# Forgetting attention and a tanh-shrink layer: q and k loaded six tokens to a partition, one DMA per tensor, and turned from there in 96x128 blocks

## The chip, the core and the metric

The kernel runs on one core of a Trainium2 chip. A core has five engines, each with an instruction queue of its own that is worked off in order: TensorE (PE in the profile; its weight loads are shown apart as PEld), VectorE (DVE), ScalarE (ACT), GpSimd (POOL) and SyncE (SP), which here only issues DMA transfers. Engines wait for one another by semaphores. Sixteen DMA engines move the data between HBM, the large memory, and SBUF, the on-chip memory of 128 partitions. TensorE writes its results into PSUM, a small memory in banks, from which VectorE and ScalarE read them.

The metric is the device time of one execution in microseconds (us). Lower is better.

## The reference

There are two parts. The first is causal attention for 8 batches of 8 heads, with 576 tokens of 64 numbers in each head; every token has a forget value f, whose logarithms are summed along the tokens and enter the scores:

```python
scores = scale * np.matmul(q, k.transpose(0, 1, 3, 2))
log_f = np.log(np.clip(f, 0.0001, 1.0))
cum = np.cumsum(log_f, axis=-1)
decay = cum[:, :, :, None] - cum[:, :, None, :]
scores = np.where(causal, -1000000000.0, scores + decay)
scores = scores - np.max(scores, axis=-1, keepdims=True)
attn = np.exp(scores)
attn = attn / (np.sum(attn, axis=-1, keepdims=True) + 1e-09)
return np.matmul(attn, v).astype(np.float32)
```

The second takes the eight heads of a token as one row of 512 numbers, 4608 tokens in all:

```python
h = x @ w_in             # 512 x 2048
g = h - np.tanh(h)
return g @ w_out         # 2048 x 512
```

All inputs and the output are float32.

## The kernel before, in words

**Attention.** The heads are worked two at a time: pair c of batch b holds heads 2c and 2c+1, and there are 32 pairs. For each pair there are seven score tiles (`scores`, matmul at L352), kept transposed: the keys stand on the partitions and the queries along the row. A score matmul multiplies a 128-column piece of `KT` (the weights) with columns of `QT`. Both tiles have 67 rows: 64 for the head's numbers and three that carry the forget sums, so that the decay comes out of the same matmul. `QT` is [67, head, 576 tokens], `KT` the same with padding to 640. There are two of each, one for even batches and one for odd. A score tile goes to one of two PSUM banks, ScalarE turns it into exponentials `e` (L361), and GpSimd zeroes what lies above the diagonal (L371). A matmul with the values (`values`, L389) gives both the sums and the weighted values, and VectorE divides them (L398 to L400) into `xn`. SP turns `xn` by DMA transposes (L423, L425) into `XR`, where the rows of x stand with the 512 numbers on the partitions.

**The layer.** Tiles of 512 tokens, u = 0 to 8. `mlp1` is 16 steps for each tile: four matmuls of `win` with `XR` (L451) into a bank `hps`, on ScalarE the tanh of -h into one of two buffers `th` (L456), and on VectorE the sum of both, `gq` (L462). `mlp2` multiplies g with w_out. From tile 1 on this is done by seven products of quarters in place of eight; their operands are sums of quarters of g, made by VectorE (`sums`, L484), and of w_out (`weights`, L278, once). The products are matmuls at L517.

**The order.** All five queues are written out by hand, in the order in which the program issues. For pair p the function `att_items` makes a list of items: the seven score tiles with what belongs between them, and at each place (p, item) the entries that a table `LOADS` has there. Steps of the layer, seven or eight a pair, are dealt out evenly between these items. So the place in `LOADS` sets where a load, a transpose or a copy stands in its engine's queue.

**How q and k come in.** They lie in HBM as [batch, head, token, 64] in float32, and are needed with the 64 numbers on the partitions, in 16 bits. Batches 0 to 2 go another way than the others: `load_qk` (L102) puts six tokens one behind the other on each of 96 partitions, TensorE turns them into PSUM (L298), and copies place them from there (L309 on ScalarE, L311 on VectorE). These copies handle even and odd tokens apart, and write every second column.

From batch 3 on (`FAR = 3`), these are the steps, for each of q and k:

- `load_block` (L108), five times: GpSimd issues a DMA that puts 128 tokens (at last 64) on the partitions, one token of all eight heads to a partition, and turns float32 into 16 bits on the way. Each of its pieces is one token of one head, 64 numbers or 256 bytes in HBM.
- `turn_block` (L113), five times: SP issues a DMA transpose of such a block. In the result, `TQ` or `TK` ([128, 4, 576]), the two heads of a pair stand on partitions 0 to 63 and 64 to 127, and the tokens along the row in their order. There are two tiles `TQ`, and one `TK`.
- `place`: copies of 64 partitions into `QT` and `KT`. For K they are four copies on VectorE (L120) of two heads each: heads 0 and 2, then 1 and 3, then 4 and 6, then 5 and 7. For Q, ScalarE copies heads 0 to 3 one at a time (L118), and VectorE heads 4 and 6, then 5 and 7 (L120). A copy reads and writes 576 tokens in a row.

The places of the copies are these lines, where b is the batch that the copies are for, p0 is the first pair of the batch ahead of it, and p0 + 4 the first pair of batch b:

```python
on_k = (p0 + 3, 0), (p0 + 3, 2), (p0 + 4, 1), (p0 + 4, 4)
if b == FAR:
    on_k = (p0 + 3, 2), (p0 + 3, 4), (p0 + 4, 0), (p0 + 4, 4)
```

For batches 4 to 7 the first two K copies thus stand at items 0 and 2 of the pair ahead of the batch, for batch 3 at items 2 and 4. The Q copies of ScalarE stand at items 3 to 6 of the first pair of the batch before (for batch 3: 1 to 4 of the pair just ahead), and those of VectorE one pair later at items 1 and 3.

Of the kernel before, what the change touches and what calls it, by code (L numbers as in the profile page):

```python
# [17 lines left out]
FAR = 3  # L18
# [3 lines left out]
def kernel(  # L22
# [10 lines left out]
    nc = tc.nc  # L33
    P = 128

    B, H, S, D = q.shape
    NH = B * H
    DM, DFF = moe_w_in.shape
# [3 lines left out]
    NJ = 5  # L42
    NT6 = 6
# [32 lines left out]
    def keep():  # L76
        while M_AT[0] % 3 in KEPT:
            M_AT[0] += 1
        KEPT.append(M_AT[0] % 3)
# [11 lines left out]
    qraw = [qkp.tile([P, H * S * D // (S // NT6)], FP16, tag=f"qn{i}", name=f"qn{i}") for i in range(2)]  # L91
    kraw = [qkp.tile([P, H * S * D // (S // NT6)], FP16, tag=f"kn{i}", name=f"kn{i}") for i in range(2)]
    qn, kn = ([t[0:S // NT6, :].rearrange("p (h n d) -> p h n d", h=H, n=NT6) for t in raw] for raw in (qraw, kraw))
    qb, kb = ([t[:, 0:NJ * DM].rearrange("p (n e) -> p n e", n=NJ) for t in raw] for raw in (qraw, kraw))
    vn = [qkp.tile([P, NJ, H, VW], FP16, tag=f"vn{i}", name=f"vn{i}") for i in range(2)]
    QT = [qkp.tile([D + 3, H, S], FP16, tag=f"QT{i}", name=f"QT{i}") for i in range(2)]
    KT = [qkp.tile([D + 3, H, PITCH], FP16, tag=f"KT{i}", name=f"KT{i}") for i in range(2)]
    TQ = [qkp.tile([P, NPAIR, S], FP16, tag=f"TQ{i}", name=f"TQ{i}") for i in range(2)]
    TK = qkp.tile([P, NPAIR, S], FP16, tag="TK", name="TK")
# [3 lines left out]
            out=dst[b % 2][:, h0:h1, :, :].rearrange("p h n d -> p h (n d)"),  # L103
            in_=src[b, h0:h1, :, :].rearrange("h (p n) d -> p h (n d)", n=NT6))

    def load_block(dst, src, b, n):
        pn = min(P, S - n * P)
        nc.gpsimd.dma_start(out=dst[b % 2][0:pn, n, :].rearrange("p (h d) -> p h d", h=H),  # L108
                            in_=src[b, :, n * P:n * P + pn, :].rearrange("h p d -> p h d"))

    def turn_block(dst, src, b, n):
        pn = min(P, S - n * P)
        nc.sync.dma_start_transpose(out=dst[:, :, n * P:n * P + pn], in_=src[b % 2][0:pn, n, :])  # L113

    def place(dst, src, b, a, c, n, eng):
        to, of = dst[b % 2][0:D, 2 * c + a:2 * c + a + 2 * n - 1:2, 0:S], src[a * D:(a + 1) * D, c:c + n, :]
        if eng == "A":
            nc.scalar.activation(out=to, in_=of, func=AF.Copy)  # L118
        else:
            (nc.gpsimd if eng == "P" else nc.vector).tensor_copy(out=to, in_=of)  # L120

    def load_v_rest(b):
        nc.gpsimd.dma_start(out=vn[b % 2][0:S % P, NJ - 1, :, 0:D],
# [115 lines left out]
    def add(where, fn, *args):  # L239
        LOADS.setdefault(where, []).append(lambda: fn(*args))  # L240

    for b in range(2, B):
        p0 = (b - 1) * NPAIR
        at_q = [(p0 - 2, n + 2) for n in range(NJ)]
        at_k = [(p0, n) for n in range(NJ)]
        at_v = [(p0 + (1 if b >= FAR else 2), n) for n in range(NJ)]
        to_q, to_k = (p0 - 1, 1), (p0 + 1, 4)
        on_q = p0
        on_k = (p0 + 3, 0), (p0 + 3, 2), (p0 + 4, 1), (p0 + 4, 4)
        if b == FAR:  # L250
            at_q = [(p0 - 1, n + 1) for n in range(NJ)]
            to_q, on_q = (p0, 4), p0 + 3
            on_k = (p0 + 3, 2), (p0 + 3, 4), (p0 + 4, 0), (p0 + 4, 4)
        add((p0, 0), load_aug, b)
        for n in range(NJ):
            if n < NJ - 1:
                add(at_v[n], load_v_block, b, n, 0, H)
            else:
                add(at_v[n], load_v_rest, b)
            if b < FAR:  # L260
                continue
            add(at_q[n], load_block, qb, q, b, n)
            add(at_k[n], load_block, kb, k, b, n)
            add(to_q, turn_block, TQ[b % 2], qb, b, n)
            add(to_k, turn_block, TK, kb, b, n)
        if b < FAR:
            add((p0, 2), load_qk, qn, q, b, 0, H)
            add((p0, 5), load_qk, kn, k, b, 0, H)
            continue
        for n, (c, a) in enumerate(((0, 0), (0, 1), (2, 0), (2, 1))):  # L270
            add(on_k[n], place, KT, TK, b, a, c, 2, "V")
            add((on_q, (1 if b == FAR else 3) + n), place, QT, TQ[b % 2], b, a, c // 2, 1, "A")
            if c:
                add((on_q + 1, 1 + 2 * a), place, QT, TQ[b % 2], b, a, c, 2, "V")

    def weights(o, x, y, n):
        ks = slice(n * NK // 2, (n + 1) * NK // 2)
# [160 lines left out]
    def widen(n):  # L438
        turn_of[:] = [n, 0]
# [218 lines left out]
    for p in range(len(pairs) + 1):  # L658
        b, c = divmod(p, NPAIR)
        items = att_items(p)  # L660
        take = TAKE[p] if p < len(TAKE) else 8 - (p - len(TAKE)) % 2
        if p == 2 * NPAIR - 1:
            keep()
        if p == 2 * NPAIR + 1:
            KEPT.clear()
            widen(1)
        mine = mlp[at:at + take]
        at += take
        first = 15 if p == NPAIR else 0
        if p == len(pairs):  # L670
            for fn, *args in mine[0:2]:
                fn(*args)
            mine = mine[2:]
        given, n = 0, 0
        whole = sum(counts for _, counts in items)
        for emit, counts in items:
            emit()
            n += counts
            while n > first and given < len(mine) and given * (whole - first) < (n - first) * len(mine):
                fn, *args = mine[given]  # L680
                fn(*args)
                given += 1
    widen(2)
    for fn, *args in mlp[at:]:
        fn(*args)
# [28 lines left out]
```

## Time and profile before

| | |
|---|---|
| median of 3 runs | 338.77 us (338.75 to 339.58) |
| span of the profiled execution | 337.1 us |
| busy: TensorE | 330.0 us (98%) |
| busy: VectorE | 260.8 us (77%) |
| busy: ScalarE | 233.2 us (69%) |
| busy: GpSimd | 163.2 us (48%) |
| DMA queue of GpSimd's transfers | 94528 packets, 18.37 MB, 75.5% of the 16 engines' span |
| DMA queue of SP's transfers | 52892 packets, 19.89 MB, 32.4% |
| granted TensorE clock | 9 tenths or more in each of 40 slices |

The busy share is the time in which an engine works at something, as a part of the span. The rest is waiting. In a row of a timeline the columns are the start (us from the span's start), the length, the engine, the line and operation, the tile written and the tiles read, and how many instructions the row joins; in brackets stands how long the engine had been idle just before, and what released it. A row of groups has the line, the engine, the operation with its shapes (partitions x elements) and its count, then the busy time and the mean in ns of one, then the idle time just ahead of such instructions and what ended most of it. In a row of the chain of waits the first two numbers are start and length.

### The profile page before, as it was taken

The page shows a single profiled execution, that of the slowest core. Times are in us where ns is not written, and L with a number is a line of the kernel's source. Part 1 is how long each engine was busy: PE and PEld are TensorE (multiplying, and loading weights), DVE is VectorE, ACT ScalarE, POOL GpSimd, SP SyncE. Part 2 cuts the span into 40 slices and gives each one's busy share as a digit, 9 for nine tenths or more (in the row PEclk, how much of TensorE's full clock was granted, in tenths as well). Part 3 has the DMA queues.
Part 4 walks back from the last instruction along what each step waited for, and adds up shares of the span by engine and source line. Part 5 has one row for each costly group of instructions (what it writes and reads, how often), then busy time and mean ns, then how long its engine had stood idle before and what let it go on. Part 6 is the DMA issues. An engine that isn't in the chain of part 4 may idle for free.

```text
span 337.1 us, 8726 instructions
## 1 busy us (share of the span) xinstructions
PE 330.0 (98%) x3313; PEld 235.6 (70%) x3313; DVE 260.8 (77%) x509; ACT 233.2 (69%) x438; POOL 163.2 (48%) x321
## 2 busy tenths in 40 slices
PE   8899999999999999999999999999999999999996
PEld 8775558875687558845888888656865686486485
DVE  7998986659887886778867896788668866966865
ACT  6997777978977886788677867787558733632630
POOL 8977467775667564767377637722322210000000
PEclk9999999999999999999999999999999999999999
DMA  9999999999979997999899999990130022002003
GB/s 113 143 203 202 186 198 165 184 159 172 142 87 190 136 134 72 164 152 139 94 122 187 118 112 117 163 132 18 51 113 2 19 65 97 2 31 95 0 12 116
DMA packets 147468, 38.82 MB, mean 115 GB/s; under 512 B 128181, under 2 KB 146335, under 8 KB 147426
## 3 DMA queue, kind: packets, MB, share of 16 engines
q0 software_dynamic: 94528, 18.37, 75.5%
q1 hardware_dynamic: 52892, 19.89, 32.4%
q8 instruction: 26, 0.43, 0.6%
q14 instruction: 16, 0.13, 0.2%
q10 hardware_dynamic: 6, 0.01, 0.0%
HBM read 36.85 MB, written 9.44 MB: 137 GB/s over the span
## 4 chain that ended last, share of the span: by engine, by line
PE 90%; DVE 7%; ACT 2%; issue 1%; ACTq 0%
PE hps L451 36%; PE ops L517 29%; PE ps L352 11%; PE av L389 8%; PE ops L492 4%; DVE KT L311 2%; DVE QT L311 1%; PE t L298 1%; ACT e L361 1%; DVE xn L400 1%; DVE gq L462 0%; DVE TQ L187 0%; ACT th L456 0%; PE x L417 0%; DVE clo L190 0%
## 5 line engine op out<-in xcount | busy, mean ns | idle before, releaser
L451 PE MATMUL hps<-XR,win 128*128 128x512 f16 (+1 forms) x640 | 140.7, 357 | 0.3 <-DVE gq L462 0.3
L456 ACT ACTIVATE th<-hps 128x512 f32<-128x512 f32 x144 | 86.6, 602 | 55.5 <-PE hps L451 53.5
L361 ACT ACTIVATE e<-ps 128x512 f16<-128x512 f32 x192 | 110.2, 597 | 8.9 <-PE ps L352 7.4
L462 DVE TENSOR_TENSOR gq<-hps,th 128x512 f16<-128x512 f32 x144 | 98.0, 687 | 23.6 <-ACT th L456 22.0
L371 POOL TENSOR_SCALAR_AFFINE_SELECT e<-e 128x128 f16<-128x128 f16 x168 | 60.7, 364 | 71.5 <-ACT e L361 68.7
L451 PEld LDWEIGHTS <-win 128*128 128x128 f16 x640 | 57.7, 97 | 49.0 <-issue 1.1
L352 PE MATMUL ps<-QT,KT 67*128 67x64 f16 (+4 forms) x384 | 76.5, 276 | 2.0 <-DVE KT L311 1.4
L517 PEld LDWEIGHTS <-gq 128*128 128x128 f16 x640 | 60.3, 97 | 11.1
L517 PE MATMUL ops<-wout,gq 128*128 128x256 f16 x512 | 63.2, 272 | 0.0
L352 PEld LDWEIGHTS <-KT 67*128 67x128 f16 x384 | 36.4, 98 | 23.4 <-DVE KT L311 2.0
L389 PEld LDWEIGHTS <-e 128*128 128x128 f16 x896 | 32.3, 97 | 3.6
L389 PE MATMUL av<-vn,e 128*128 128x65 f16 x896 | 33.6, 193 | 0.0
L517 PE MATMUL ops<-W,sq 128*128 128x256 f16 x256 | 31.2, 272 | 0.0
L131 POOL DMA_DIRECT2D vn<-in_v_dram x32 | 28.0, 877 | 6.5 <-DMA win<-in_moe_w_in_dram 2.9
L400 DVE TENSOR_TENSOR xn<-av,rs 128x640 f16<-128x640 f32 x32 | 26.4, 825 | 1.3 <-DVE rs L399 0.2
L517 PEld LDWEIGHTS <-sq 128*128 128x128 f16 x256 | 24.1, 97 | 3.4
L108 POOL DMA_DIRECT2D kn<-in_k_dram x25 | 21.2, 848 | 2.1 <-issue 1.8
L108 POOL DMA_DIRECT2D qn<-in_q_dram x25 | 21.2, 848 | 1.8 <-issue 1.4
L371 POOL TENSOR_SCALAR_AFFINE_SELECT el<-el 128x128 f16<-128x128 f16 x28 | 9.3, 333 | 26.1 <-ACT el L361 25.8
L398 DVE TENSOR_SCALAR rs<-av 128x10 f32<-128x10 f32 x32 | 5.2, 163 | 18.2 <-PE av L389 17.0
L532 ACT ACTIVATE m<-ops 128x512 f32<-128x512 f32 x16 | 9.5, 596 | 10.9 <-PE ops L517 10.9
L484 DVE TENSOR_TENSOR gq<-gq 128x512 f16<-128x512 f16 x32 | 17.1, 533 | 0.0
(83 smaller groups left out, 311.8 us busy)
## 6 DMA issues: line engine op xcount, KB each, us to landing
out_dram<-ost SPq DMA_DIRECT2D x34, 256.0 KB
vn<-in_v_dram POOLq DMA_DIRECT2D x24, 128.0 KB, 6.2
qn<-in_q_dram POOLq DMA_DIRECT2D x20, 128.0 KB, 5.0
kn<-in_k_dram POOLq DMA_DIRECT2D x20, 128.0 KB, 5.6
win<-in_moe_w_in_dram POOLq DMA_DIRECT2D x2, 1024.0 KB, 11.8
wout<-in_moe_w_out_dram POOLq DMA_DIRECT2D x2, 1024.0 KB, 15.6
XR<-xn SPq DMA_TRANSPOSE x56
qn<-in_q_dram POOLq DMA_DIRECT2D x6, 144.0 KB, 4.6
```

What stands on the lines that cost most here:

```text
L108: nc.gpsimd.dma_start(out=dst[b % 2][0:pn, n, :].rearrange("p (h d) -> p h d", h=H), in_=src[b, :, n * P:n * P + pn, :].rearrange("h p d - ...
L131: nc.gpsimd.dma_start(out=vn[b % 2][:, n, h0:h1, 0:D], in_=v[b, h0:h1, n * P:(n + 1) * P, :].rearrange("h p d -> p h d"))
L352: nc.tensor.matmul(out=ps[:, col:col + n], lhsT=kt[0:rows, h, j * P:(j + 1) * P], rhs=qt[0:rows, h, i0:i0 + n], start=True, stop=cut == 0)
L361: nc.scalar.activation(out=e[:, lo:hi], in_=ps[:, lo:hi], func=AF.Exp, bias=-SHIFT, scale=qscale)
L371: nc.gpsimd.affine_select(out=view, in_=view, compare_op=ALU.is_ge, fill=0.0, base=0, pattern=pat, channel_multiplier=-1)
L389: nc.tensor.matmul(out=av[:, a, ib, :], lhsT=E.pop((b, c, a, j, ib)), rhs=vn[b % 2][:, j, 2 * c + a, 0:D + 1], start=(j == 0), stop=(j == ib))
L400: nc.vector.tensor_tensor(out=xn.rearrange("p i (a d) -> p a i d", a=2), in0=av[:, :, :, 0:D], in1=rs.to_broadcast([P, 2, NJ, D]), op=ALU. ...
L451: nc.tensor.matmul(out=hps[:, o:o + n], lhsT=win[:, ci, ft * P:(ft + 1) * P], rhs=XR[:, ci, t:t + n], start=(ci == 0), stop=(ci == NCH - 1))
L456: nc.scalar.activation(out=th, in_=hps, func=AF.Tanh, scale=-1.0)
L462: nc.vector.tensor_tensor(out=GQ[(u, i)][:, half, kt, :], in0=hps, in1=th, op=ALU.add)
L484: nc.vector.tensor_tensor(out=LHS[name](u, i)[:, ks], in0=LHS[x](u, i)[:, ks], in1=LHS[y](u, i)[:, ks], op=op)
L517: nc.tensor.matmul(out=ps[:, m, :], lhsT=LHS[lhs](u, kt // 4)[:, kt % 4, m * P:(m + 1) * P], rhs=rhs[:, kt, :], start=(fresh and (apart or ...
```

## The change

For batches 3 to 7, q and k are now loaded as in batch 2: `load_qk` for all eight heads, one DMA for each tensor. Each of its pieces is six tokens of one head, 1536 bytes in HBM, and it ends on 96 partitions of a raw tile, with (head, token of six, number) along the row.

`turn_raw` (L109 of the new kernel) then issues two DMA transposes for each tensor, one for heads 0 to 3 and one for heads 4 to 7. Each turns twelve blocks of 96 partitions by 128 columns. A block holds two neighbouring tokens (64 numbers each) of one head, so in `TQ` and `TK` the even tokens now stand on partitions 0 to 63 and the odd ones on 64 to 127, and the row of a head is three stretches of 96 (one for each of the three pairs of tokens among the six).

`place` takes one parity e of the tokens, of as many heads as it is told. For each stretch element it reads one of each of the three stretches, 96 elements apart, and writes them to every second column of `QT` or `KT`. The count of copies and of elements in each is as before, with other shares: K's four copies on VectorE (L118) are now the even tokens of heads 0 to 3, the odd tokens of heads 0 to 3, then the same of heads 4 to 7. ScalarE's four Q copies (L116) are even and odd of heads 0 and 1, then of heads 2 and 3; VectorE's two are even and odd of heads 4 to 7. The places of the copies in `LOADS` are the same as before. The loads have one place where they had five.

```diff
-    def load_block(dst, src, b, n):
-        pn = min(P, S - n * P)
-        nc.gpsimd.dma_start(out=dst[b % 2][0:pn, n, :].rearrange("p (h d) -> p h d", h=H),
-                            in_=src[b, :, n * P:n * P + pn, :].rearrange("h p d -> p h d"))
-
-    def turn_block(dst, src, b, n):
-        pn = min(P, S - n * P)
-        nc.sync.dma_start_transpose(out=dst[:, :, n * P:n * P + pn], in_=src[b % 2][0:pn, n, :])
-
-    def place(dst, src, b, a, c, n, eng):
-        to, of = dst[b % 2][0:D, 2 * c + a:2 * c + a + 2 * n - 1:2, 0:S], src[a * D:(a + 1) * D, c:c + n, :]
+    def blocks(t):
+        return t.rearrange("p c (g r) -> p (c g) r", r=S // NT6)
+
+    def turn_raw(dst, src, b, h0, h1):
+        nc.sync.dma_start_transpose(out=blocks(dst)[:, 3 * h0:3 * h1, :],
+                                    in_=src[b % 2][0:S // NT6, h0 * NT6 * D:h1 * NT6 * D])
+
+    def place(dst, src, b, h0, h1, e, eng):
+        to = dst[b % 2][0:D, h0:h1, e:S:2].rearrange("d h (r g) -> d h r g", g=NT6 // 2)
+        of = blocks(src)[e * D:(e + 1) * D, 3 * h0:3 * h1, :].rearrange("d (h g) r -> d h r g", g=NT6 // 2)
...
-        at_q = [(p0 - 2, n + 2) for n in range(NJ)]
-        at_k = [(p0, n) for n in range(NJ)]
...
-            at_q = [(p0 - 1, n + 1) for n in range(NJ)]
...
+        at_q, at_k, to_q, to_k = (p0 - 2, 2), (p0, 1), (p0 - 1, 1), (p0 + 1, 4)
...
+            at_q, at_k, to_q, to_k = (p0 - 1, 2), (p0, 1), (p0, 4), (p0 + 1, 4)
...
-        for n, (c, a) in enumerate(((0, 0), (0, 1), (2, 0), (2, 1))):
-            add(on_k[n], place, KT, TK, b, a, c, 2, "V")
-            add((on_q, (1 if b == FAR else 3) + n), place, QT, TQ[b % 2], b, a, c // 2, 1, "A")
-            if c:
-                add((on_q + 1, 1 + 2 * a), place, QT, TQ[b % 2], b, a, c, 2, "V")
+        add(at_q, load_qk, qn, q, b, 0, H)
+        add(at_k, load_qk, kn, k, b, 0, H)
+        for n in range(2):
+            add(to_q, turn_raw, TQ[b % 2], qraw, b, 4 * n, 4 * n + 4)
+            add(to_k, turn_raw, TK, kraw, b, 4 * n, 4 * n + 4)
+        for n in range(4):
+            m, e = divmod(n, 2)
+            add(on_k[n], place, KT, TK, b, 4 * m, 4 * m + 4, e, "V")
+            add((on_q, (1 if b == FAR else 3) + n), place, QT, TQ[b % 2], b, 2 * m, 2 * m + 2, e, "A")
+            if m:
+                add((on_q + 1, 1 + 2 * e), place, QT, TQ[b % 2], b, 4, H, e, "V")
```

In the fences below each row is one instruction, or as many as its count says: the line, the operation, the tile written and those read, and the shape; a number behind a tile's name tells apart tiles that share a name. The orders of TensorE and ScalarE are the same in both kernels, but for the line numbers and the shapes of ScalarE's copies.

VectorE around the first scores of batch 3, before. `KT_106` is the K tile of odd batches, the rows from `rs` to `xn` are the division of the pair before, and `sq` are sums of quarters of g:

```order
L120 COPY KT_106<-TK 64x2x576
L398 TENSOR_SCALAR rs<-av 128x10
L399 RECIPROCAL rs<-rs 128x10
L400 TENSOR_TENSOR xn<-av,rs 128x2x5x64
L484 TENSOR_TENSOR sq<-gq 128x512 x4
L484 TENSOR_TENSOR sq<-sq,gq 128x512
L120 COPY KT_106<-TK 64x2x576
```

and after:

```order
L118 COPY KT_106<-TK 64x4x288
L395 TENSOR_SCALAR rs<-av 128x10
L396 RECIPROCAL rs<-rs 128x10
L397 TENSOR_TENSOR xn<-av,rs 128x2x5x64
L481 TENSOR_TENSOR sq<-gq 128x512 x4
L481 TENSOR_TENSOR sq<-sq,gq 128x512
L118 COPY KT_106<-TK 64x4x288
```

The order is the same. What a copy holds has changed: two whole heads before, one parity of four heads after.

GpSimd around the load of q for a batch, before. `qn_97` is the raw tile of q for even batches, and the rows at L371 zero what lies above the diagonal in the exponentials:

```order
L108 DMA qn_97<-in_q_dram 128x8x64
L371 AFFINE_SELECT el_137<-el_137 128x128
L108 DMA qn_97<-in_q_dram 128x8x64
L371 AFFINE_SELECT e<-e 128x128
L108 DMA qn_97<-in_q_dram 128x8x64
L371 AFFINE_SELECT e<-e 128x128
L108 DMA qn_97<-in_q_dram 128x8x64
L371 AFFINE_SELECT e<-e 128x2x128
L108 DMA qn_97<-in_q_dram 64x8x64
```

and after, from the same place:

```order
L101 DMA qn_97<-in_q_dram 96x8x384
L368 AFFINE_SELECT el_137<-el_137 128x128
L368 AFFINE_SELECT e<-e 128x128 x2
L368 AFFINE_SELECT e<-e 128x2x128
L368 AFFINE_SELECT e<-e 128x128 x2
```

The whole load now stands where the first of its five parts stood, and the other four places are empty.

SP around the transposes of q for an odd batch (`TQ_108`), with those of `XR` ahead of and behind them, before:

```order
L425 DMA_TRANSPOSE XR<-xn 128x64
L113 DMA_TRANSPOSE TQ_108<-qn_98 128x4x128 x4
L113 DMA_TRANSPOSE TQ_108<-qn_98 128x4x64
L423 DMA_TRANSPOSE XR<-xn 128x4x128
L425 DMA_TRANSPOSE XR<-xn 128x64
```

and after:

```order
L422 DMA_TRANSPOSE XR<-xn 128x64
L109 DMA_TRANSPOSE TQ_108<-qn_98 128x12x96 x2
L420 DMA_TRANSPOSE XR<-xn 128x4x128
L422 DMA_TRANSPOSE XR<-xn 128x64
```

Two transposes stand where five stood. Each of them waits for the one load.

More of the change, by code (lines that the diff above doesn't have):

```diff
@@ L93 @@
     qn, kn = ([t[0:S // NT6, :].rearrange("p (h n d) -> p h n d", h=H, n=NT6) for t in raw] for raw in (qraw, kraw))
-    qb, kb = ([t[:, 0:NJ * DM].rearrange("p (n e) -> p n e", n=NJ) for t in raw] for raw in (qraw, kraw))
     vn = [qkp.tile([P, NJ, H, VW], FP16, tag=f"vn{i}", name=f"vn{i}") for i in range(2)]
@@ L119, in place @@
         else:
-            (nc.gpsimd if eng == "P" else nc.vector).tensor_copy(out=to, in_=of)
+            nc.vector.tensor_copy(out=to, in_=of)
     def load_v_rest(b):
@@ L243 @@
         p0 = (b - 1) * NPAIR
-        at_q = [(p0 - 2, n + 2) for n in range(NJ)]
-        at_k = [(p0, n) for n in range(NJ)]
[L246 to L250, printed above, removed]
-            at_q = [(p0 - 1, n + 1) for n in range(NJ)]
-            to_q, on_q = (p0, 4), p0 + 3
-            on_k = (p0 + 3, 2), (p0 + 3, 4), (p0 + 4, 0), (p0 + 4, 4)
+        late_b = b >= FAR
+        at_v = [(p0 + (1 if late_b else 2), n) for n in range(NJ)]
         add((p0, 0), load_aug, b)
@@ L259 @@
                 add(at_v[n], load_v_rest, b)
[L260 to L266, printed above, removed]
+        if not late_b:
             add((p0, 2), load_qk, qn, q, b, 0, H)
@@ L269 @@
             continue
-        for n, (c, a) in enumerate(((0, 0), (0, 1), (2, 0), (2, 1))):
-            add(on_k[n], place, KT, TK, b, a, c, 2, "V")
-            add((on_q, (1 if b == FAR else 3) + n), place, QT, TQ[b % 2], b, a, c // 2, 1, "A")
-            if c:
-                add((on_q + 1, 1 + 2 * a), place, QT, TQ[b % 2], b, a, c, 2, "V")
+        at_q, at_k, to_q, to_k = (p0 - 2, 2), (p0, 1), (p0 - 1, 1), (p0 + 1, 4)
+        on_q = p0
+        on_k = (p0 + 3, 0), (p0 + 3, 2), (p0 + 4, 1), (p0 + 4, 4)
+        if b == FAR:
+            at_q, at_k, to_q, to_k = (p0 - 1, 2), (p0, 1), (p0, 4), (p0 + 1, 4)
+            on_q = p0 + 3
+            on_k = (p0 + 3, 2), (p0 + 3, 4), (p0 + 4, 0), (p0 + 4, 4)
+        add(at_q, load_qk, qn, q, b, 0, H)
[9 more added lines that the diff above has]
+                add((on_q + 1, 1 + 2 * e), place, QT, TQ[b % 2], b, 4, H, e, "V")
     def weights(o, x, y, n):
@@ L682 @@
                 given += 1
+        assert given == len(mine)
     widen(2)
```

## The prediction

> **What bounds the kernel now.** I read the page's busy shares first, then the chain that ended last, then the windows of one batch, and then the timelines at the places where the edited copies stand.
>
> ```profile
> PE 330.0 (98%) x3313; PEld 235.6 (70%) x3313; DVE 260.8 (77%) x509; ACT 233.2 (69%) x438; POOL 163.2 (48%) x321
> 108.79 1.73 PE hps L451 x8
> 281.69 13.81 PE hps L451 x64
> 130.90:166.30 35.40, 35.40 (x347) 24.25 (x346) 27.29 (x56) 26.52 (x53) 22.36 (x43) 1.00 1.45 133
> 166.30:201.80 35.50, 35.50 (x411) 30.47 (x409) 27.28 (x56) 26.52 (x53) 22.32 (x43) 1.00 1.47 131
> ```
>
> The first row is the page's, the next two are pieces of the chain, the last two are windows of one batch each (length, then the busy time of PE, PEld, DVE, ACT and POOL, the granted clock, the DMA engines' share in them, GB/s). TensorE is busy in all of both batches, at clock 1.00, and not only nominally: eight 512-column matmuls in the middle of attention take 1.73 us (216 ns each), and 64 of them at the end, with no attention beside them, 13.81 us (216 ns each). TensorE is at its pace; nothing that the change lightens (loads, GpSimd's issues) stands in front of it. So I look for what could make TensorE wait. VectorE is idle for 8.1 us of a batch and ScalarE for 8.9 us, and both stand in TensorE's loops.
>
> **The change part by part.** Loads: 50 issues (25 a tensor) on GpSimd become 10, and the transposes on SP fall from 50 to 20. Both engines get time back, which is worth nothing where TensorE doesn't wait for them. What the change adds is in the placing copies, as many as before (30 on VectorE, 20 on ScalarE) with the same number of elements, but now reading steps of 96 elements and writing every second element.
>
> ```profile
> L120 DVE COPY KT<-TK 64x1152 f16<-64x1152 f16 x20 | 9.4, 470 | 0.3
> L311 DVE COPY QT<-t 64x576 f16<-64x576 f16 x18 | 14.4, 800 | 2.2 <-PE t L298 2.1
> L311 DVE COPY KT<-t 64x288 f16<-64x288 f16 x4 | 1.9, 477 | 0.1
> L419 DVE COPY XR<-x 128x576 f16<-128x576 f16 x2 | 0.9, 456 | 0.6 <-PE x L417 0.5
> L118 ACT ACTIVATE QT<-TQ 64x576 f16<-64x576 f16 x20 | 13.7, 683 | 0.5
> L309 ACT ACTIVATE QT<-t 64x576 f16<-64x576 f16 x4 | 3.3, 817 | 0.1
> L421 ACT ACTIVATE XR<-x 128x576 f16<-128x576 f16 x2 | 1.3, 654 | 0.0
> ```
>
> These are groups by line and shape (busy, mean ns). No row shows the new form, from SBUF with both steps; L311 and L309 have the same steps, from PSUM.
>
> *VectorE's copy.* L311 gives (800 - 477) / 288 = 1.12 ns an element and 154 ns fixed. At that pace 1152 elements take 1.44 us, the upper end. The old copy's 0.47 us, where steps cost nothing, is the lower end. It moves 1152 / (470 - 154) = 3.6 elements in a ns, four times L311's pace. [...] I take the middle of 0.80 and 1.44, 1.12 us, since L311 is the nearest in form and L120 in place: 0.67 us more than the 0.44 to 0.46 us that a single copy takes in the timelines below.
>
> [...]
>
> *ScalarE's copy.* Steps cost 817 - 654 = 163 ns for 576 elements out of PSUM (L309 against L421). I add that to L118's 0.68: 0.85 us. The lower end is 0.68; the upper is VectorE's ratio for the same two tiles, 800 / 456 = 1.75, hence 1.20 us. I take 0.85, the row of the same engine and shape.
>
> Term 1, **the first scores of batch 3**. Before, one copy placed all tokens of heads 0 and 2, and the next all of heads 1 and 3. Now one places the even tokens of heads 0 to 3 and the next the odd tokens, so head 0 needs both. VectorE's timeline, and TensorE's row with that score (the last of the x3):
>
> ```profile
> 91.22 0.69 DVE L462 TENSOR_TENSOR gq<-hps,th 128x512 f16<-128x512 f32 x1 [0.73 <-ACT th L456]
> 91.83 0.44 DVE L120 COPY KT<-TK 64x1152 f16<-64x1152 f16 x1
> 92.20 0.15 DVE L398 TENSOR_SCALAR rs<-av 128x10 f32<-128x10 f32 x1
> ...
> 93.38 1.51 DVE L484 TENSOR_TENSOR sq<-gq 128x512 f16<-128x512 f16 x4
> 94.81 0.41 DVE L484 TENSOR_TENSOR sq<-sq,gq 128x512 f16<-128x512 f16 x1
> 95.24 0.46 DVE L120 COPY KT<-TK 64x1152 f16<-64x1152 f16 x1
> 94.68 0.71 PE L352 MATMUL ps<-QT,KT 67*128 67x320 f16 x3
> ```
>
> The score starts at 94.68 + 0.71 - 0.38 = 95.01, before the second copy even begins. With the first copy 0.67 longer, the gq ahead of it up to 0.16 later (it waits for ScalarE, which has a stepped copy ahead), and nothing idle in between, the second begins at 96.07, ends at 97.19, and the score follows perhaps 0.1 later (the weight load and the hop): a wait of 2.3 us. With unchanged copies it is 95.70 + 0.1 - 95.01 = 0.8; with 0.80 us copies 1.6; with 1.44 us copies 2.9. TensorE's queue is in order, so all behind it waits too, and no later idle time can give it back. In batches 4 to 7 the table of places has both copies of the first heads two items earlier. VectorE's second one and TensorE's row with the first score of batch 5:
>
> ```profile
> 161.33 0.46 DVE L120 COPY KT<-TK 64x1152 f16<-64x1152 f16 x1
> 165.52 0.60 PE L352 MATMUL ps<-QT,KT 67*128 67x320 f16 x3
> ```
>
> [...]
>
> Term 2, **ScalarE between the scores of a batch's first pair** (batches 4 to 7, once each). Four Q copies stand there between the exponentials:
>
> ```profile
> 136.01 0.68 ACT L118 ACTIVATE QT<-TQ 64x576 f16<-64x576 f16 x1
> 136.86 0.60 ACT L361 ACTIVATE e<-ps 128x512 f16<-128x512 f32 x1 [0.17 <-PE ps L352]
> 137.48 0.68 ACT L118 ACTIVATE QT<-TQ 64x576 f16<-64x576 f16 x1
> 138.07 0.57 ACT L361 ACTIVATE e<-ps 128x512 f16<-128x512 f32 x1
> 138.67 0.68 ACT L118 ACTIVATE QT<-TQ 64x576 f16<-64x576 f16 x1
> 139.26 0.57 ACT L361 ACTIVATE e<-ps 128x512 f16<-128x512 f32 x1
> 139.86 0.68 ACT L118 ACTIVATE QT<-TQ 64x576 f16<-64x576 f16 x1
> 140.45 1.70 ACT L361 ACTIVATE e<-ps 128x512 f16<-128x512 f32 x3
> 139.89 0.38 PE L352 MATMUL ps<-QT,KT 67*128 67x448 f16 x2
> 141.07 0.38 PE L352 MATMUL ps<-QT,KT 67*128 67x320 f16 x2
> ```
>
> Score tiles have two banks, so each score waits for the exponential two before it. The exponential of 139.26 ends at 139.83 and the score starts at 139.89; the first of 140.45 ends near 141.02 (0.57 us as its neighbours) and the score starts at 141.07. TensorE is already on ScalarE's heels there. The copy at 136.01 has 0.17 us of idle time behind it and swallows its 0.16; the other three arrive in full: 4 batches x 3 x 0.163 = 2.0 us. Ends: 0, and 4 x 3 x 0.51 = 6.1 us. Batch 3's Q copies fall in front of term 1's wait and are covered by it.
>
> Term 3, **Q copies between the sums of g**:
>
> ```profile
> 146.41 0.46 DVE L120 COPY QT<-TQ 64x1152 f16<-64x1152 f16 x1
> 146.90 1.43 DVE L462 TENSOR_TENSOR gq<-hps,th 128x512 f16<-128x512 f32 x2
> 148.09 0.60 ACT L456 ACTIVATE th<-hps 128x512 f32<-128x512 f32 x1
> ```
>
> The th at 148.09 takes the buffer that the first of these gq reads (two buffers). That gq ends near 147.59; 0.67 later is 148.26, so ScalarE starts up to 0.2 late and hands it to the next score. Four batches give 0.7 us. The other VectorE copies have the 8.1 us of idle time a batch against 6 x 0.67 = 4.0 us, and I cost them at nothing; were they 1.35 us longer each, that cover would be gone. Ends: 0, and 2 us with 1.44 us copies.
>
> The DMA side I cost at nothing. The first block of q that now becomes the whole load was issued at 117.14 for a copy that stands at 136.01:
>
> ```profile
> 117.14 0.89 POOL L108 DMA_DIRECT2D qn<-in_q_dram  x1 [0.41 <-issue]
> qn<-in_q_dram POOLq DMA_DIRECT2D x1, 576.0 KB, 14.6
> qn<-in_q_dram POOLq DMA_DIRECT2D x6, 144.0 KB, 4.6
> ```
>
> A quarter of such a load lands in 4.6 us. The one of 14.6 us was issued right behind a megabyte of weights, which isn't there later. Somewhere from 6 to 9 us is my estimate between these rows, so SP waits a few us at each Q transpose; behind it in its queue stand XR's transposes, issued a pair later.
>
> Sum: 2.3 + 2.0 + 0.7 = 5.0 us. The profiled span of 337.1 becomes 342.1. The median of the runs shown is 338.77, 1.67 us above the span, and becomes 343.8 us, 1.5% slower. I count 0.3% (1.0 us) as what a measurement of this kernel can tell from no change.
>
> **The rivals.**
> A: ScalarE pays 1.75 as VectorE does out of PSUM, copies near 1.20 us. Term 2 is 6.1, term 1 some 0.3 larger: 338.8 + 9.4 = 348.2. For it, the ratio of L311 to L419; against it, L309 itself at 817.
> [...]
> B: steps are free, copies stay at 0.46 and 0.68. Then only 0.8 us of term 1 is left: 339.6, no change that can be told. It decides as long as all copies together add under 0.2 us to terms 1 to 3. For it, the old copies are in SBUF; against it, every stepped row is slower than its plain neighbour.
> [...]
> D: the load lands as late as 14.6 us. 117.14 + 14.6 and a transpose of 2 to 6 us passes 136.01 by up to 2 us, in four batches: about 352. Against it, the weights ahead of that row.
> E: fewer DMAs free something that TensorE waits for. TensorE has no gap to give from 100 us on; at most 1 us, 338.
>
> **How the numbers follow.** The forecast with its own range of 341.5 to 346 (0.80 to 1.44 us copies) has 0.53; A 0.21, B 0.09, C 0.08, D 0.04, E 0.02, something unnamed and slower 0.03. The predicted time is the forecast's 343.8. The range goes from 340.3 (1.6 us: term 1 with 0.80 us copies and ScalarE's free) to 349.8 (A with 1.44 us copies gives 2.9 + 6.1 + 2.0 = 11.0): it leaves out B, C, D and E, and takes most of A. Faster 0.02 (E), same 0.09 (B), slower 0.89.
>
> **What would show it.** In the profile after: VectorE's placing copies at 0.8 to 1.4 us and ScalarE's near 0.85; one wait of TensorE for VectorE's KT copy near 95 us, 1.6 to 2.9 long, and none like it in later batches; L352's waits for L361 grown by half a us at the first pair of batches 4 to 7; GpSimd's busy time some 35 us less, with no use. The prediction is wrong if the copies stay under 0.5 us, if ScalarE's pass 1 us, if TensorE waits for XR or a transpose, or if the wait at 95 us is missing.

## The result, and the profile after

The changed kernel takes 342.06 us (median, 342.02 to 343.02), against 338.77 before: 1.0101 times as long, with an interval of 1.0085 to 1.0117. The profiled execution has a span of 340.3 us, 3.2 more than before.

First the page of the kernel after: TensorE's busy time, GpSimd's, the score matmuls (the last entry is the idle time ahead of them and what ended most of it), the placing copies, and from the groups by shape VectorE's copies of Q.

```profile
PE 332.0 (98%) x3313; PEld 236.8 (70%) x3313; DVE 269.7 (79%) x509; ACT 235.8 (69%) x438; POOL 133.5 (39%) x281
q0 software_dynamic: 55488, 18.36, 52.7%
L349 PE MATMUL ps<-QT,KT 67*128 67x64 f16 (+4 forms) x384 | 76.6, 276 | 3.0 <-DVE KT L118 1.5
L116 ACT ACTIVATE QT<-TQ 64x576 f16<-64x576 f16 x20 | 17.1, 853 | 0.5
L118 DVE COPY KT<-TK 64x1152 f16<-64x1152 f16 x20 | 16.8, 842 | 0.3
L118 DVE COPY QT<-TQ 64x1152 f16<-64x1152 f16 x10 | 8.3, 830 | 0.2
```

GpSimd has 30 us less to do (35 were forecast), and its DMA queue takes 52.7% of the engines' span where it took 75.5%. Nobody was waiting for either. The copies have grown from 0.47 to 0.84 us on VectorE and from 0.68 to 0.85 on ScalarE. TensorE's row names a new wait, for the K copies.

To find where the 3.2 us came in, I took the start of each matmul in both traces and looked for the places where the distance grows (TensorE's order is the same in both, so each has its partner):

| place (time before) | distance grows by |
|---|---|
| first score of batch 3, head 0 (95.0 us) | 1.53 us |
| scores of the first pair of batches 4, 5, 6 and 7 (the last ones near 105, 140, 176 and 211 us) | 0.36 us each: 0.02, 0.22, 0.12 |
| all other places from 10 us to the last matmul | 0.04 us together |

That makes 3.02 us. The other 0.2 us of the span lie behind TensorE's last matmul and SP's last issue.

The first place, in the timelines of VectorE and TensorE after:

```profile
91.96 0.81 DVE L118 COPY KT<-TK 64x1152 f16<-64x1152 f16 x1
92.66 0.15 DVE L395 TENSOR_SCALAR rs<-av 128x10 f32<-128x10 f32 x1
...
95.28 0.41 DVE L481 TENSOR_TENSOR sq<-sq,gq 128x512 f16<-128x512 f16 x1
95.70 0.80 DVE L118 COPY KT<-TK 64x1152 f16<-64x1152 f16 x1
96.56 0.39 PE L349 MATMUL ps<-QT,KT 67*128 67x512 f16 x1 [1.48 <-DVE KT L118]
```

The second copy starts at 95.70 (95.24 before), ends at 96.50, and the score starts at 96.56, where it started at 95.01.

The second kind of place, in ScalarE's and TensorE's timelines for the first pair of the batch whose rows the prediction showed:

```profile
138.77 0.60 ACT L358 ACTIVATE e<-ps 128x512 f16<-128x512 f32 x1
139.39 0.85 ACT L116 ACTIVATE QT<-TQ 64x576 f16<-64x576 f16 x1
140.12 0.56 ACT L358 ACTIVATE e<-ps 128x512 f16<-128x512 f32 x1
140.70 0.85 ACT L116 ACTIVATE QT<-TQ 64x576 f16<-64x576 f16 x1
141.43 0.56 ACT L358 ACTIVATE e<-ps 128x512 f16<-128x512 f32 x1
142.01 0.85 ACT L116 ACTIVATE QT<-TQ 64x576 f16<-64x576 f16 x1
142.73 1.68 ACT L358 ACTIVATE e<-ps 128x512 f16<-128x512 f32 x3
140.48 0.62 PE L349 MATMUL ps<-QT,KT 67*128 67x320 f16 x3
142.04 0.38 PE L349 MATMUL ps<-QT,KT 67*128 67x448 f16 x2
143.34 0.38 PE L349 MATMUL ps<-QT,KT 67*128 67x320 f16 x2
```

ScalarE goes without a pause. From one exponential to the next it takes 1.31 and 1.30 us (140.12, 141.43, 142.73), where it took 1.19 (138.07, 139.26, 140.45). The scores follow at 142.04 and 143.34; the score of 142.04 starts as the exponential of 141.43 ends (141.99). So each stepped copy puts ScalarE another 0.12 us behind. The first of the three scores had 0.1 us of room and starts 0.02 late; the next two have none, and start 0.22 and 0.12 later still: 0.36 together.

The place of term 3 and the loads, from ScalarE's and VectorE's timelines and the DMA view:

```profile
148.68 0.82 DVE L118 COPY QT<-TQ 64x1152 f16<-64x1152 f16 x1
149.53 1.29 DVE L459 TENSOR_TENSOR gq<-hps,th 128x512 f16<-128x512 f32 x2
150.36 0.60 ACT L453 ACTIVATE th<-hps 128x512 f32<-128x512 f32 x1
qn<-in_q_dram POOLq DMA_DIRECT2D x6, 576.0 KB, 6.8
kn<-in_k_dram POOLq DMA_DIRECT2D x6, 576.0 KB, 9.6
```

The th that stood at 148.09 stands at 150.36, 2.27 later, as much as all of TensorE's work has moved there (1.53 + 2 x 0.36 = 2.25). The longer copy ahead of it adds nothing.

### The profile page after: what moved, and what is told of

Its sections match the earlier page's. It is cut to its first block, busy times and chain, and to the rows that moved or that the text cites. A ratio compares the mean times of both kernels' runs of the same rounds, so it can differ in the third digit from the quotient of the medians.

```text
span 340.3 us, 8584 instructions
## 1 busy us (share of the span) xinstructions
PE 332.0 (98%) x3313; PEld 236.8 (70%) x3313; DVE 269.7 (79%) x509; ACT 235.8 (69%) x438; POOL 133.5 (39%) x281
## 3 DMA queue, kind: packets, MB, share of 16 engines
q0 software_dynamic: 55488, 18.36, 52.7%
## 4 chain that ended last, share of the span: by engine, by line
PE 87%; DVE 7%; ACT 4%; issue 1%; ACTq 0%
PE hps L448 35%; PE ops L514 26%; PE ps L349 11%; PE av L386 7%; PE ops L489 4%; ACT e L358 2%; PE idle L563 2%; DVE KT L308 2%; PE t L295 1%; DVE QT L308 1%; DVE gq L459 1%; DVE xn L397 1%; ACT th L453 1%; ACT QT L116 1%; DVE sq L481 1%
## 5 line engine op out<-in xcount | busy, mean ns | idle before, releaser
L368 POOL TENSOR_SCALAR_AFFINE_SELECT e<-e 128x128 f16<-128x128 f16 x168 | 63.7, 381 | 101.0 <-ACT e L358 99.4
L116 ACT ACTIVATE QT<-TQ 64x576 f16<-64x576 f16 x20 | 17.1, 853 | 0.5
L118 DVE COPY KT<-TK 64x1152 f16<-64x1152 f16 x20 | 16.8, 842 | 0.3
L308 DVE COPY KT<-t 64x576 f16<-64x576 f16 (+1 forms) x20 | 14.7, 736 | 2.7 <-PE t L295 2.1
```

Of the source, the lines that this page charges most:

```text
L308: nc.vector.tensor_copy(out=to, in_=of)
L368: nc.gpsimd.affine_select(out=view, in_=view, compare_op=ALU.is_ge, fill=0.0, base=0, pattern=pat, channel_multiplier=-1)
```

## The experiments

The theory from the two traces: all of the loss is in the placing copies. 1.53 us come from the two stepped K copies that batch 3's first score needs, 0.36 us in each of four batches from ScalarE's Q copies. The rivals: late loads or transposes; VectorE's longer copies, in other places than that one; and for each of the two terms another split of its size.

**Loads and transposes alone.** The changed kernel with the placing copies of before. Their tokens stand in the wrong places, so this is a kernel for its time alone.

```diff
-    def place(dst, src, b, h0, h1, e, eng):
-        to = dst[b % 2][0:D, h0:h1, e:S:2].rearrange("d h (r g) -> d h r g", g=NT6 // 2)
-        of = blocks(src)[e * D:(e + 1) * D, 3 * h0:3 * h1, :].rearrange("d (h g) r -> d h r g", g=NT6 // 2)
+    def place(dst, src, b, a, c, n, eng):
+        to, of = dst[b % 2][0:D, 2 * c + a:2 * c + a + 2 * n - 1:2, 0:S], src[a * D:(a + 1) * D, c:c + n, :]
```

> The new loads and the new transposes, with the placing copies of before (whole rows of 576, two heads on VectorE, one on ScalarE); the copies put the tokens in wrong places. Theory (the copies carry all of the loss): no change from before, 338.5 to 339.1, copies back at 0.47 and 0.68 us, no wait of TensorE for a K copy near 95 us. Rival (loads or transposes come late and are what is waited for): 340 to 342, with the wait near 95 us still there.

The time is 339.1 us against 338.8, ratio 1.001 (1.0001 to 1.0019). TensorE's score stands where it stood before, without a wait:

```profile
94.70 0.71 PE L347 MATMUL ps<-QT,KT 67*128 67x320 f16 x3
```

From 120 us to the end each matmul starts within a hundredth of a us of its time before. So TensorE waits neither for the 576 KB loads nor for the two transposes, and what they save is not gained either. The profiled span is 0.2 us longer all the same; this lies behind TensorE's last matmul, as in the changed kernel, and no run shows what it is.

**The wait near 95 us.** Two kernels: batch 3's first K copies sooner, and VectorE's copies plain but still split so that head 0 needs both.

```diff
-            on_k = (p0 + 3, 2), (p0 + 3, 4), (p0 + 4, 0), (p0 + 4, 4)
+            on_k = (p0 + 3, 0), (p0 + 3, 2), (p0 + 4, 0), (p0 + 4, 4)
```

> The changed kernel with batch 3's first two K copies at items 0 and 2 of the pair ahead, as in the other batches, instead of 2 and 4. Theory (TensorE waits for the second of the two stepped copies, 1.53 us once): that wait goes and 0.34 us a batch for ScalarE stays, 342.06 - 1.53 = 340.5 (340.2 to 340.8). Rival (K's transposes for batch 3 land too late to place earlier): VectorE waits for them, 342 or more.

341.11 us, 1.0067 (1.0052 to 1.0082): about 0.95 us of the 1.53 is gained, not all. In the trace the first score of batch 3 still starts 0.45 us late. TensorE's and ScalarE's rows there:

```profile
95.47 0.38 PE L349 MATMUL ps<-QT,KT 67*128 67x512 f16 x1 [0.40 <-DVE sq L481]
94.86 0.56 ACT L358 ACTIVATE e<-ps 128x512 f16<-128x512 f32 x1
```

The second K copy had ended at 92.9. The trace puts the rest of the wait down to a sum on VectorE, but the exponential ends at 95.42, and the score tile of two before is its buffer. The kernel with plain ScalarE copies and early K, below, decides this.

```diff
+        if eng in "V":
+            to = dst[b % 2][0:D, h0:h1, 0:S].rearrange("d h (n x) -> d h n x", x=64)[:, :, :, 32 * e:32 * e + 32]
+            of = blocks(src)[e * D:(e + 1) * D, 3 * h0:3 * h1, :].rearrange("d (h g) r -> d h (g r)", g=NT6 // 2).rearrange("d h (n x) -> d h n x", x=32)
```

> The changed kernel with VectorE's placing copies reading whole rows and writing runs of 32 (tokens in wrong places), head 0's scores still needing both of the first two; ScalarE's as changed. Theory (the wait near 95 us is the split by parity, 0.8 us, plus 0.35 for each of the two copies): copies near 0.47 to 0.6 us, the wait falls to 0.8 to 1.0, 341.4 (341.1 to 341.7). Rival (the length of the copies alone makes the wait): it goes, 340.5. Rival (late data): it stays at 1.5, 342.0.

341.38 us, 1.0079 (1.0064 to 1.0095). The copies and TensorE's wait:

```profile
L121 DVE COPY KT<-TK 64x1152 f16<-64x1152 f16 x20 | 9.2, 460 | 0.3
PE ps L352 <- DVE KT L121: 0.8, 1, 0.8
```

So of the 1.53 us, 0.85 (the growth of the distance at this score) are the split by parity: even copies as short as before would make the score wait for the second of them. The other 0.68 are the copies' length.

**ScalarE's copies.** The same lines with `if eng in "A"`, first in the changed kernel, then with the early K as well.

> The changed kernel with ScalarE's Q copies reading whole rows and writing runs of 32 in a row (tokens in wrong places), VectorE's as changed. Theory (four batches lose 0.34 us each because ScalarE's copies grew from 0.68 to 0.85): 342.06 - 1.36 = 340.7 (340.4 to 341.0), the wait of 1.5 us near 95 us stays. Rival (the 0.34 us a batch come from VectorE's longer copies): 342.0, no change.

340.73 us, 1.0055 (1.0038 to 1.0072): 1.33 us gained. The 0.36 us a batch are gone from all four batches, and the wait near 95 us stays (1.5 us):

```profile
L119 ACT ACTIVATE QT<-TQ 64x576 f16<-64x576 f16 x20 | 13.6, 682 | 0.5
PE ps L352 <- DVE KT L121: 1.4, 1, 1.4
```

> The changed kernel with batch 3's first K copies at items 0 and 2, and ScalarE's Q copies plain (tokens in wrong places); VectorE's stepped as changed. Theory (0.45 us that stayed near 95 us with early K are ScalarE's four stepped copies of batch 3, and VectorE's longer copies cost nothing where they aren't waited for): 338.9 (338.6 to 339.2). Rival (the 0.45 are VectorE's sums of g, pushed back by the moved copy, as the release by sq in the table of waits has it): 339.3 to 339.6.

339.12 us, 1.0008 (0.9999 to 1.0017): no difference from before that can be told. The 0.45 us are gone, with VectorE's sums as they were; so they were ScalarE's. The name of the releaser in the row above was wrong. And VectorE's 30 copies are still the long ones, and cost nothing:

```profile
L121 DVE COPY KT<-TK 64x1152 f16<-64x1152 f16 x20 | 17.1, 856 | 0.3
```

With this the loss is taken apart: the split and the K copies near 95 us, ScalarE's Q copies elsewhere, and the 0.2 us behind the last matmul that came with the loads.

**Reading or writing.** The copies read 96 apart and write every second element. Three kernels have one of these alone, or the other order of the elements (reading runs of 96, writing every sixth; its tokens are right, those of the other two are not).

```diff
-        to = dst[b % 2][0:D, h0:h1, e:S:2].rearrange("d h (r g) -> d h r g", g=NT6 // 2)
+        to = dst[b % 2][0:D, h0:h1, e * (S // 2):(e + 1) * (S // 2)].rearrange("d h (r g) -> d h r g", g=NT6 // 2)
```

> The changed kernel with all placing copies reading 96 apart as changed, but writing without a step (each parity's 288 tokens of a head in a row, so in wrong places). Only the length of the copies counts here. If the reading's hops make the copies longer: 0.8 us on VectorE, 0.85 on ScalarE. If the writing's step does, as the 2.1 us of the copies that wrote every sixth element suggest: 0.47 and 0.68.

```diff
-        to = dst[b % 2][0:D, h0:h1, e:S:2].rearrange("d h (r g) -> d h r g", g=NT6 // 2)
-        of = blocks(src)[e * D:(e + 1) * D, 3 * h0:3 * h1, :].rearrange("d (h g) r -> d h r g", g=NT6 // 2)
+        to = dst[b % 2][0:D, h0:h1, e:S:2]
+        of = blocks(src)[e * D:(e + 1) * D, 3 * h0:3 * h1, :].rearrange("d (h g) r -> d h (g r)", g=NT6 // 2)
```

> The changed kernel with all placing copies reading in a row and writing every second element (tokens in wrong places). If the writing's step makes the copies longer: 0.8 us on VectorE and 0.85 on ScalarE, and the time of the changed kernel, 342.0. If the reading's hops do: 0.47 and 0.68, and 339.7.

```diff
-        to = dst[b % 2][0:D, h0:h1, e:S:2].rearrange("d h (r g) -> d h r g", g=NT6 // 2)
-        of = blocks(src)[e * D:(e + 1) * D, 3 * h0:3 * h1, :].rearrange("d (h g) r -> d h r g", g=NT6 // 2)
+        to = dst[b % 2][0:D, h0:h1, e:S:2].rearrange("d h (r g) -> d h g r", g=NT6 // 2)
+        of = blocks(src)[e * D:(e + 1) * D, 3 * h0:3 * h1, :].rearrange("d (h g) r -> d h g r", g=NT6 // 2)
```

> The changed kernel, same tokens in the same places, but each copy goes through its elements in the other order: it reads runs of 96 in a row and writes every sixth element, instead of reading 96 apart and writing every second. If the hops of the reading are what costs: copies near 0.5 us on VectorE and 0.68 on ScalarE, the wait near 95 us falls to 0.85 and ScalarE's 0.34 a batch go, 339.7. If the steps of the writing cost: copies stay at 0.82 and 0.85 or get longer, 342.0 or more.

The groups of the copies. Reading 96 apart alone:

```profile
L116 ACT ACTIVATE QT<-TQ 64x576 f16<-64x576 f16 x20 | 15.4, 769 | 0.5
L118 DVE COPY KT<-TK 64x1152 f16<-64x1152 f16 x20 | 15.0, 750 | 0.3
```

Writing every second alone:

```profile
L116 ACT ACTIVATE QT<-TQ 64x576 f16<-64x576 f16 x20 | 17.1, 854 | 0.5
L118 DVE COPY KT<-TK 64x1152 f16<-64x1152 f16 x20 | 16.8, 840 | 0.3
```

Reading runs, writing every sixth:

```profile
L116 ACT ACTIVATE QT<-TQ 64x576 f16<-64x576 f16 x20 | 42.7, 2133 | 0.5
L118 DVE COPY KT<-TK 64x1152 f16<-64x1152 f16 x20 | 42.4, 2122 | 0.3
```

One run each gave 340.59 us for the first and 342.13 for the second; the third is 380.79, 1.1225 times before (1.1204 to 1.1246). That time holds more than the copies: the granted TensorE clock was 0.955 in the mean of the profiled run (about 34 us at 0.50, worked out from that mean), of which the last section says more. I had put it as the one or the other, and it is neither: each alone makes the copy longer, and both together are as long as the longer of the two. The writing with a step of two decides, and a step of six costs three times a plain copy on ScalarE (0.68) and four and a half times on VectorE (0.47).

Why writing every sixth is so much slower than writing every second (2.12 us against 0.84 on VectorE), and why reading 96 apart costs less than either (0.75), no run here shows.

**What VectorE's idle time covers.** The order of the last kernel on VectorE alone, with ScalarE's copies plain, gives copies of 2.12 us, 1.65 longer than before; by the prediction's account idle time covers them until they are 1.35 longer.

> VectorE's placing copies at 2.12 us (reading in runs of 96, writing every sixth element; tokens right), ScalarE's plain (tokens in wrong places). [...] By the prediction's account (idle time of VectorE, 8.1 us a batch, covers six copies until they are 1.3 us longer each): term 1 grows to about 4.1 us, and 6 x 1.66 - 8.1 = 1.9 us in each of four batches, 338.8 + 4.1 + 7.5 = 350.4 (347 to 354). Rival (VectorE's idle time lies in pieces between sums of g, and a copy that is longer than a piece makes TensorE wait at once): each of some 26 copies costs about 1 us, 360 to 370. Other rival (the buffers of g let VectorE fall behind by a few us and catch up): 343 to 345, term 1 alone.

362.48 us, 1.0704 (1.0686 to 1.0722). Its table of waits, and the window of one batch (length, then busy time of PE, PEld, DVE, ACT and POOL):

```profile
PE ps L352 <- ACT e L361: 7.9, 9, 1.5
PE ops L517 <- DVE ost L536: 4.6, 5, 1.2
PE ps L352 <- DVE KT L121: 4.1, 1, 4.1
PE hps L451 <- DVE ost L536: 2.5, 4, 0.7
140.90:180.20 39.30, 35.84 (x346) 24.17 (x345) 36.54 (x56) 26.33 (x52) 24.50 (x35) 1.00 0.86 119
```

The wait of term 1 is 4.1, as worked out. It has a sequel that nobody had worked out: the granted clock falls to 0.57 in the four us behind it (the column ahead of the DMA share),

```profile
99.00:103.00 4.00, 3.61 (x18) 2.41 (x19) 3.97 (x6) 1.19 (x2) 1.62 (x2) 0.57 0.03 7
```

and matmuls of 256 columns follow one another every 213 ns there instead of 109, which loses 1.6 us more (worked out from the two paces over some 3.3 us). And a full batch takes 39.3 us, 3.9 more than before, and not 1.9: VectorE still has 2.8 us idle in it. TensorE loses most of that in waits for sums behind a long copy (1.4 us between 140 and 176), and for exponentials (2.1 us). So the idle time is not one store from which copies can be paid; part of it lies where no copy can use it. The rival with pieces was nearer in kind, though each of the 28 other copies costs (23.7 - 4.1 - 1.6) / 28 = 0.64 us and not 1.

**Looking for a version that beats both.** First, the Q copies of ScalarE for batches 4 to 7 given to VectorE, whose copy moves twice the elements in the same time (1152 in 0.84 us, ScalarE's 576 in 0.85), and ScalarE's for batch 3 one pair sooner.

```diff
-            add((on_q, (1 if b == FAR else 3) + n), place, QT, TQ[b % 2], b, 2 * m, 2 * m + 2, e, "A")
+            if b == 3:
+                add((p0 + 2, 1 + n), place, QT, TQ[b % 2], b, 2 * m, 2 * m + 2, e, "A")
+            elif not m:
+                add((on_q, 3 + 2 * e), place, QT, TQ[b % 2], b, 0, 4, e, "V")
```

> The changed kernel with early K, ScalarE's four Q copies of batches 4 to 7 made by VectorE in two (heads 0 to 3, one parity each, at items 3 and 5), and those of batch 3 on ScalarE one pair earlier. Theory (ScalarE was the one that TensorE waited for, and VectorE has the room: 8 us idle a batch before, 2 of them taken, and 1.6 more now): 338.6 (338.2 to 339.2). Rival (VectorE is full by then, and the sums of g come late): 340 or more.

With early K as well, 340.95 us, 1.006 (1.0045 to 1.0075). In batches 5 to 7 it does a little better than the kernel before: one score in each comes 0.1 us sooner, as the small wait of TensorE for ScalarE is gone there, and 0.15 us in all are left of it at the end. It loses where the copies land on a busy stretch. TensorE's rows:

```profile
87.67 0.38 PE L352 MATMUL ps<-QT,KT 67*128 67x512 f16 x1 [1.00 <-ACT e L361]
106.45 1.03 PE L517 MATMUL ops<-wout,gq 128*128 128x256 f16 x8 [0.52 <-DVE ost L536]
```

The first is batch 3's Q copies, sooner, among ScalarE's tanh; the second is batch 4's, on VectorE among batch 3's K copies and the sums. The rival had the second; the first, the larger, is a wait for ScalarE, which neither the theory nor the rival had.

Then batch 2 as well by the new way, which takes 48 transposes from TensorE:

```diff
-FAR = 3
+FAR = 2
...
+        if b == 2:
+            at_q, at_k, to_q, to_k = (p0, 1), (p0, 4), (p0 + 2, 1), (p0 + 2, 5)
...
-            if p in (2 * NPAIR - 1, 2 * NPAIR) and ti % 2 == 0:
-                pair = pairs[2 * NPAIR + 2 * (p - 2 * NPAIR + 1) + ti // 4]
-                put(trans, *pair, *((kn, KT) if ti % 4 else (qn, QT)), False, "VA")
```

> As the last one, and batch 2 too is loaded in two DMAs and turned by DMA transposes, so that TensorE has 48 transposes of some 40 ns fewer (1.9 us) and its third bank of the layer from pair 7 on; batch 2's copies stand in pair 7. Theory (TensorE is at its pace, so what is taken from it is gained): 336.8 (336 to 337.6). Rival (the loads land too late in the busy stretch before 60 us, or SP's queue holds up XR's transposes): 339 or more.

> Batch 2 too by two DMAs and DMA transposes, as in the kernel that waited for K's transposes near 60 us, but with those transposes ten us sooner in SP's queue and the K copies three items later; batch 3's and 4's Q copies on ScalarE as changed, those of batches 5 to 7 on VectorE, early K for batch 3. Theory (what TensorE no longer does is gained once the data is there): 338.83 + 0.45 + 0.34 - 0.28 - 1.9 = 337.4 (336.8 to 338.4). Rival (the DMA engines are full before 60 us and the transposes land late wherever they stand): 341 or more, with a wait for K's transposes on VectorE.

352.32 us (1.0409, 1.0367 to 1.0452), and with the transposes sooner 348.56 (1.0283, 1.0254 to 1.0312). SP's, VectorE's and TensorE's rows of the second:

```profile
53.74 7.86 SPq L109 DMA_TRANSPOSE TK<-kn  x2
64.66 1.61 DVE L118 COPY KT<-TK 64x1152 f16<-64x1152 f16 x2 [9.09 <-DMA TK<-kn]
66.33 0.61 PE L356 MATMUL ps<-QT,KT 67*128 67x512 f16 x1 [4.95 <-DVE KT L118]
```

K's transposes are issued from 53.74 on, and the copies can start only at 64.66. In the first of the two kernels they were issued at 57.42 and waited for until 67.83. The four us by which SP came sooner (ten were meant) brought three at the copies. So it came as the rival had it, 341 or more with a wait for K's transposes. Its reason, DMA engines that are full, isn't shown: why a transpose takes ten us in this stretch, while those of later batches are in time, is open. The share of the DMA engines there is below that of the kernel before (the last column but one, first before, then this kernel):

```profile
50.00:60.00 10.00, 9.89 (x126) 8.38 (x125) 6.33 (x12) 7.82 (x14) 7.54 (x15) 1.00 2.03 165
```

```profile
50.00:60.00 10.00, 7.35 (x87) 6.00 (x86) 3.59 (x8) 4.78 (x10) 3.60 (x9) 1.00 1.49 161
```

But the transposes are not alone in being late there. GpSimd's loads of v, issued between 44 and 51 us, took this long to land (the last number, a median in us; first before, then this kernel):

```profile
vn<-in_v_dram POOLq DMA_DIRECT2D x4, 128.0 KB, 12.5
vn<-in_v_dram POOLq DMA_DIRECT2D x4, 128.0 KB, 17.0
```

What the K copies of this kernel wait for is the one thing that would have to be mended first. No kernel was found that beats the one before.

## Why the prediction was right, and where it was off

**What bounds the kernel**: right. TensorE was at its pace; fewer issues, transposes and packets gave nothing, as the run with the loads alone shows (339.1). The loads land in 6.8 and 9.6 us, where 6 to 9 was the estimate, and no wait of TensorE came of it.

**Direction and mechanism**: right. The two largest terms are at the two places named, and the batch 3 score waits for the second K copy, as it would not in any later batch. That ScalarE's Q copies of batch 3 are covered by that wait is shown too: with the wait taken away, 0.45 us of theirs come out.

**Size**: 5.0 us were forecast and 3.2 came, of the profiled spans; by the medians 3.29. Each of the three terms was too large.

- *VectorE's copy* was the step that failed most: "I take the middle of 0.80 and 1.44 ... since L311 is the nearest in form and L120 in place". It is 0.84 in the mean, 0.81 at the place of term 1. The lower of the two was right as a number; the pace of a copy out of PSUM (1.12 ns an element, 1.44 us) did not carry over to one inside SBUF. The 0.80 was my estimate, 154 + 576 x 1.12 ns: L311's pace for half of the elements. No run shows that half of them is what counts, and none shows the middle of 1.12 us that went into the sum: the runs had 0.75 for reading 96 apart, 0.84 for writing every second, and 2.12 for writing every sixth. With 0.80 the prediction's own working gave 1.6 for term 1, and 1.53 was measured.
- *Term 2* was 2.0 and came to 4 x 0.36 = 1.4. The copy's length was right (0.85 forecast, 853 ns measured). The mistake was to add the difference of two lengths, 0.163. ScalarE's rows overlap: before, a copy and an exponential were 0.68 + 0.57 long, but came every 1.19 us, not 1.25. From start to start the stepped copy adds 0.12, and 3 x 0.12 is the 0.36.
- *Term 3* was 0.7 and came to nothing. The step there was 0.67 on a copy; with 0.36, the sum of g still ends ahead of the tanh that needs its buffer.

**VectorE's other copies at nothing**: the amount was right (the run with plain ScalarE copies and early K: 339.12). The reason given was too simple. By it, copies of 2.12 us should have cost 11.6 us, and they cost 23.7: idle time summed over a batch is an upper bound of what can be covered.

**The rivals**: A fell with ScalarE's 853 ns, B with every copy; D's condition did not come up (the loads landed in 6.8 and 9.6 us); E gave nothing.

## What to carry to other kernels

When a transfer is made cheaper by a layout that later has to be undone, price the undoing on the engines that stand in the bound engine's loop, and ask of each first use whether it now needs two copies where it needed one: here the split by parity alone was 0.85 us. Measure what an instruction adds from the start of one to the start of the next, not by its length (0.12 us here, not 0.163), and don't take the pace of a strided copy out of PSUM for one inside SBUF (here 1.44 us by that pace, and 0.84 measured). Where a copy must step, try the order in which the writing has the smaller step: here 0.84 us with a step of two, 2.12 with one of six.

## What was not expected of the hardware

A copy of 64x1152 16-bit elements inside SBUF on VectorE took 0.46 us plain, 0.75 reading 96 elements apart, 0.84 writing every second, 0.84 with both, and 2.12 writing every sixth; on ScalarE, half as many elements took 0.68, 0.77, 0.85, 0.85 and 2.13. With the step of six the two engines need the same time for one copy, though ScalarE's has half the elements.

Waits of TensorE cost more than their length in some of these kernels. After the 4.1 us wait of the kernel with slow VectorE copies, matmuls of 256 columns came every 213 ns for some 3.3 us, and then every 109 ns again. After the 1.5 us wait of the changed kernel they came every 109 ns at once. My working of a 4 us wait had not taken this in.

The granted clock fell also without a wait as long as 4.1 us. In the kernel that writes every sixth element on both engines, no wait is longer than 2.2 us, and the clock's mean over the run was 0.955. Here is one stretch of half clock, 6.82 us long, and the 3.41 us ahead of it (length, TensorE's busy time first, the granted clock ahead of the last two columns):

```profile
157.52:160.93 3.41, 1.58 (x12) 1.10 (x12) 3.35 (x4) 3.36 (x5) 2.35 (x2) 1.00 0.26 84
160.93:167.75 6.82, 6.26 (x52) 4.46 (x49) 2.94 (x5) 3.26 (x4) 5.54 (x7) 0.50 0.60 70
```

Nor did the length of a wait tell alone. In the first kernel with batch 2 by the new way, after a wait of 2.40 us, the next eight matmuls of 256 columns took 1.89 us where they took 1.04 before it, and the granted clock from 60 to 70 us was 0.50. In the second, after a wait of 2.54 us, they took 1.04 as before it; there the clock fell only behind the next wait, of 4.95 us, and eight took 1.91.
